# Attention and MLP on one core: the next unit's key part and its copies asked for half a step sooner, and the second pair's bias tiles asked for in units 2 and 3

## The chip, the core and the metric

One NeuronCore of a Trainium2 chip (trn2). Its engines run side by side, each through its own list of instructions in order: TensorE (PE, with its weight loads shown as PEld), VectorE (DVE), ScalarE (ACT), GpSimd (POOL) and SyncE (SP). They wait for each other through semaphores. DMAs are issued here by SP and, for the query part, by POOL. The metric is the device time of one execution in microseconds (us).

## What is computed

Attention over 4 batches, 8 heads, 576 positions and a head size of 64, with a position bias that a small network computes, followed by a two-layer network on the 2304 tokens:

```python
scores = scale * np.matmul(q, k.transpose(0, 1, 3, 2))
h = np.maximum(x @ w1 + b1, 0.0)          # x: log distance over log position, per pair of positions
bias = h @ w2                             # one value per head
scores = scores + bias.transpose(2, 0, 1)[None, :, :, :]
scores = scores - np.max(scores, axis=-1, keepdims=True)
attn = np.exp(scores)
attn = attn / (np.sum(attn, axis=-1, keepdims=True) + 1e-09)
out = np.matmul(attn, v)
...
h = x @ w_in                              # 2304 x 512 by 512 x 2048
g = np.where(h >= 1, h, np.where(h <= -1, 0.0, (h + 1) ** 2 / 4))
y = g @ w_out                             # 2304 x 2048 by 2048 x 512
```

All values are float32. The kernel splits the operands of most products into a rounded high part and a remainder, the low part, and adds the products of the parts.

## The kernel before

**Stages.** From 0 to about 70 us the bias is computed for all heads and stored to DRAM (`bias_d`). From about 70 to 345 us the attention runs. The rest is the two-layer network (lines L678 to L710), with its weights and the start of its input prepared while the attention ends.

**Units, pairs and steps.** The attention is a loop over 16 units. Unit n is one pair of heads (p = n // 4) and one batch (b = n % 4), so the first pair is units 0 to 3 and the second is units 4 to 7. A unit works through five row blocks, k = 0 to 4: four of 128 rows for both heads, and one (named `S_L`, `e_L`, `T_L`) with the last 64 rows of both. For each block:

- TensorE makes the scores S from the keys and the query (L431 and L432; L452 and L453 for the last block), into one of two buffers in PSUM;
- DVE adds the bias tile and finds the row maximum (L434, L454), which frees the buffer;
- ACT takes the exponential (L441);
- TensorE transposes e (T, L497), and the result is split into hi and lo. For some pieces ACT and DVE do that (L472, L473). For five pieces a unit ACT copies T to a tile c (L477), DVE or POOL makes hi (L481 on DVE, L479 on POOL), and POOL subtracts: lo = c - hi (L482). Those five are the second head of block 0, both heads of block 2 and both heads of block 3. POOL makes hi itself for block 0 and for the first head of block 3.

The value products O (L535, L537) are made per half unit, first from hi and then from lo, for the first head and then for the second. The second half of unit n (blocks 2, 3 and the last; tiles `hi_1` and `lo_1`) is multiplied in the first part of unit n + 1.

**The parts of the next units.** `prep(n)` gives eight steps for unit n: 0, load the raw keys and queries (`qk`, L157, on SP); 1, load the query part twice (`qa`, L153, issued by POOL); 2, load the values (`v`, L165, on SP); 3, the high part of the keys (`kh`, a DVE copy, L149); 4, the high part of the values (`vs`, DVE, L161); 5 and 6, the remainder `ls` of the keys in two column halves (POOL, L131), each followed by two DMAs on SP that copy the remainder into the query tile (L176) and the high part of the keys into the other 64 partitions (L177); 7, the remainder of the values (POOL, L131). The scores of unit n need the copies of steps 5 and 6.

**What sets the order.** `CFG["t"]` gives each step a time. A unit has ten half-steps, two per row block, the first behind the block's scores and the second behind its transposes. A time from 0 to 9 places the step of unit n at that half-step of unit n - 2, a time from 10 to 19 at that half-step less 10 of unit n - 1. `STEPS` sorts them, and `step` (called twice per block) runs those that are due. For unit 1, the steps with a time under 10 run during the bias stage. `LB` gives for the five bias tiles of the next pair the batch and the block at which each is asked for; tile 4 is `biasL`. A scheduler then orders each engine's instructions by what it holds to be ready and may move one ahead of where the program has it. On POOL the instructions that go through the helper `pool` keep their program order in the loop; the DVE copies of steps 3 and 4 are kept in order only outside it (`early`). On SP a DMA that waits holds up all behind it.

```python
if t == 20 - 10 * m + i_ and 0 < n + m < N:
    preps[n + m][i]()
```

Of the kernel before, what the change touches and what calls it, by code (L numbers as in the profile page):

```python
# [24 lines left out]
NG = S // 16  # L25
# [3 lines left out]

CBW = (1, 1, 32, C, C, C * H, S // 4, NG)  # L30
CB = sum(CBW)
CFG = dict(un=('paaa',) * NG, xa=((((14, 0), (14, 1), '', 'p'), ((14, 2), (14, 4), '', 'p'), ((14, 4), (15, 0), '', 'p'), ((14, 3), (15, 1), 'bias', 'p')), (((15, 0), (15, 1), 'kh', 'p'), ((15, 0), (15, 2), 'kl', 'v'), ((15, 1), (15, 3), 'vs', 'p'), ((15, 1), (15, 4), '', 'v'))), ex=(9, 2, 0, 2, 9), bb=5, mv=1, hi='pvvpv', rb='a', lag=(1, 1), dr=(3, 1, 2, 2, 2), pool=((0, 1), (2, 0), (2, 1), (3, 0), (3, 1)), sb=4, keep=1, drain=2, diag='a', rb2='v', eps='v', rc=2, rbb=1, hb=2, rawb=(2, 2), t=(3, 10, 11, 10, 18, 11, 12, 19), eb=4, seq=0, pb=(6, 9, 12, 14, 16), pq=22, tb=6, ub=12, low0='ppp', anch=(8, 8, 16, 23, 23), low1='ppp', ob=6, gb=3, fin=2, wt=((15, 1), (15, 4)), lastp=15, xs=2, sbf=('v', 'v', 'v', 'v', 'v'), bsE=(), ytail='p')
EPS = 1e-9
RB = 2
LASTP = CFG["lastp"]
XA = CFG["xa"]
NX = [((14, 0), (14, 1), (14, 1), (15, 0)), ((4, 0), (6, 0), (8, 0), (10, 0))]
WT = CFG["wt"]
LB = ((1, 1), (2, 1), (3, 2), (3, 3), (2, 3))
POOL, SB, KEEP, RBB = CFG["pool"], CFG["sb"], CFG["keep"], CFG["rbb"]  # L40
STEPS = sorted((t, i) for i, t in enumerate(CFG["t"]))
BIG = 3.0e38
# [4 lines left out]
def attn_cpb_moe_kernel(ctx, tc, qk, vL, cb, win, wout, lw, ident, ii, out):  # L47
# [22 lines left out]
    lp = ctx.enter_context(tc.tile_pool(name="a_load", side="right", bufs=2))  # L70
    bp = loads.enter_context(tc.tile_pool(name="a_bias", side="right", bufs=CFG["bb"]))
    qp = loads.enter_context(tc.tile_pool(name="a_qkv", side="right", bufs=2))
# [116 lines left out]
    with ExitStack() as ph:  # L189
# [21 lines left out]
        diag = [ac.tile([P, P], F32, name=f"diag{i}") for i in range(2)]  # L211
# [6 lines left out]
        pq = cp.tile([P, 2, C, H], F32, name="pq")  # L218
# [110 lines left out]
    xs = {}  # L329
# [63 lines left out]
    with ExitStack() as ph:  # L393
# [8 lines left out]
        def load_bias(p, k):  # L402
            if k < 4:
                if (p, k) in ((1, 1), (2, 3)):
                    t = rps[0].tile([P, 3, TH], F32, tag="x", name=f"bias{p}_{k}", bufs=1).rearrange("p a b -> p (a b)")
                else:
                    t = bp.tile([P, 2 * S], F32, tag="bias", name=f"bias{p}_{k}")
                nc.sync.dma_start(out=t[:, 0:S], in_=bias_r[k][:, 2 * p, :])
                nc.sync.dma_start(out=t[:, S : S + D], in_=bias_r[k][:, 2 * p + 1, 512:S])
                nc.sync.dma_start(out=t[:, S + D : 2 * S], in_=bias_r[k][:, 2 * p + 1, 0:512])  # L410
            else:
                t = bp.tile([P, S], F32, tag="biasL", name=f"biasL{p}", bufs=2)
                for j in range(2):
                    nc.sync.dma_start(out=t[D * j : D * j + D, :], in_=bias_r[4][:, 2 * p + j, :])
            return t
# [72 lines left out]
        def transposes(n, k, es, eT):  # L488
            hi, lo = eT
            off = P * (k % 2)  # L490
            e = es[k]
            if k < 4:
                for j in range(2):
                    ps = psT.tile([P, 4, P], F32, tag="T", name=f"T{n}_{k}_{j}")
                    for tb in range(4):
                        c0 = 640 * j + P * tb
                        nc.tensor.transpose(ps[:, tb, :], e[:, c0 : c0 + P], id_s)  # L497
                    split(ps, hi[:, 4 * j : 4 * j + 4, off : off + P], lo[:, 4 * j : 4 * j + 4, off : off + P], EV(n, k, j), (k, j))
            else:
                ps = psT.tile([P, 4, 2, D], F32, tag="T", name=f"T{n}_L")  # L500
                for tb in range(4):
                    nc.tensor.transpose(ps[:, tb].rearrange("p a b -> p (a b)"), e[:, P * tb : P * tb + P], id_s)
                for j in range(2):
                    split(ps[:, :, j, :], hi[:, 4 * j : 4 * j + 4, 256:320], lo[:, 4 * j : 4 * j + 4, 256:320], EV(n, k, j), (k, j))
# [43 lines left out]
        bias = {0: [load_bias(0, k) for k in range(5)]}  # L548
# [4 lines left out]
        def drain(keep, mid=None, at=0):  # L553
            while len(queue) > keep:
                at -= 1
                if at == 0:
                    mid()
                for f in queue.pop(0):
                    f()
# [10 lines left out]
        def step(i_):  # L570
            store_x()
            for m in range(3):
                for t, i in STEPS:
                    if t == 20 - 10 * m + i_ and 0 < n + m < N:
                        preps[n + m][i]()

        go[0] = True
        for n in range(N):
            p, b = n // B, n % B
            if n + 2 < N:  # L580
                preps[n + 2] = prep(n + 2)
            es[n] = []
            if n >= LASTP:
                go[0] = False
            for k in range(5):
                e, later = scores(n, k, qkv[n], bias[p])
                es[n].append(e)
                exps = [False]

                def exp_():  # L590
                    if not exps[0]:
                        exps[0] = True
                        for f in later:
                            exps.append(f())

                if CFG["ex"][k] == 0:
                    exp_()
                step(2 * k)
                if p + 1 < NP:
                    for k_ in range(5):  # L600
                        if (b, k) == LB[k_]:
                            bias.setdefault(p + 1, {})[k_] = load_bias(p + 1, k_)

                def tr(n=n, k=k):
                    half = k // 2 if k < 4 else 1
                    if k in (0, 2):
                        w = 256 + D * half
                        eT[n, half] = (
                            (tp0, tp1)[half].tile([P, 9, w], F32R, tag=f"hi{half}", name=f"hi{n}_{half}"),
                            (tp0, tp1)[half].tile([P, 9, w], F32R, tag=f"lo{half}", name=f"lo{n}_{half}"),  # L610
                        )
                    transposes(n, k, es[n], eT[n, half])
                    if k in (1, 4):
                        shared(n, half, es[n], eT[n, half])

                def inv(n=n):
                    nc.vector.reciprocal(out=sums[n], in_=sums[n])

                def rc(n=n):
                    recips(n)  # L620

                if k in (1, 4):
                    def av(n=n, half=0 if k == 1 else 1):
                        values(n, half, es[n], eT[n, half], qkv[n]["v"])
                    queue.append([tr, inv] if k == 4 else [tr])
                    late.append([CFG["lag"][0 if k == 1 else 1], [av] if k == 1 else [av, rc]])
                else:
                    queue.append([tr])
                while late and late[0][0] <= 0:
                    queue.append(late.pop(0)[1])  # L630
                for x in late:
                    x[0] -= 1
                drain(CFG["dr"][k], exp_, CFG["ex"][k])
                exp_()
                last_e = exps[-1]
                step(2 * k + 1)
                for i in range(NK):
                    for j in range(2):
                        ask, make, home, e = XA[j][i]
                        if (n, k) == ask:  # L640
                            r = None
                            if home:
                                po, w, n_ = dict(kh=(qp, QW, CFG["hb"]), kl=(qp, QW, 2), vs=(qp, 10 * P, 2), bias=(bp, 2 * S, CFG["bb"]))[home]
                                r = po.tile([P, w], F32, tag=home, name=f"rx{j}_{i}", bufs=n_)
                                r = r[:, : 3 * TH].rearrange("p (a b) -> p a b", a=3)
                            xe[i, j] = split_x(0, i, j, e, r)
                        if (n, k) == make:
                            xe[i, j]()
                for f in range(2):
                    if (n, k) == WT[f]:  # L650
                        with tc.issue_after(last_e.ins):
                            weights(f)
# [166 lines left out]
```

## Time and profile before

| | |
|---|---|
| median of 3 runs | 764.74 us (762.58, 764.74, 770.16) |
| the profiled execution's own time | 770.81 us |
| its span, first to last instruction | 769.0 us |
| TensorE busy, share of the span | 717.0 us, 93% |
| ACT, DVE, POOL busy | 62%, 58%, 55% |
| mean granted clock of TensorE, as a share of full speed | 0.984 |
| attention, units 0 to 15 | about 70 to 345 us |
| scores waiting for kh<-kh | 4.2 us in 4 waits |

The profile is one execution. Times in it are us from the span's start. A timeline row is: start, duration, engine, line and operation, out<-in by the program's names, shapes, how many instructions were merged (x4), and in brackets how long the engine had been idle before and for what. For several merged instructions the duration is that of the whole run. SPq is SP's issuing of DMAs, and the duration there is that of the issue, not of the transfer. A busy TensorE row is modelled from starts, so starts are what to compare.

### The profile page before, as it was taken

Reading aid. Unit: us, or ns where it says so; the run is one execution under the profiler, and the core shown is the slowest. Engines: PE = TensorE matmul, PEld = TensorE weight load, DVE = VectorE, ACT = ScalarE, POOL = GpSimd, SP = SyncE. Lnnn points to the kernel's source line nnn. Section 1 sums busy time; section 2 is a strip of 40 time slices with the busy share of each in tenths; the row PEclk is TensorE's granted clock in tenths of the full one; section 3 lists DMA queues with packets and bytes.
Section 4 is the critical chain, followed back from the end, with each engine's and each line's share of the span. In section 5 each row is a group of like instructions: output and inputs, shape, how many; then the busy total and the mean of one; then the engine's idle time right before and its main releaser. Section 6 shows DMA issues by size and latency. Waiting matters only on the chain. (4 is left out here: it accounts for less than half of the span.)

```text
span 769.0 us, 13382 instructions
## 1 busy us (share of the span) xinstructions
PE 717.0 (93%) x4688; PEld 635.8 (83%) x4688; DVE 445.7 (58%) x907; ACT 475.1 (62%) x1041; POOL 419.6 (55%) x362
## 2 busy tenths in 40 slices
PE   5677899899999999787899999999999999999997
PEld 2324899899999999775888889999998999989996
DVE  6998788778878888574665734663222243222222
ACT  7996889879989899596798562432222243222222
POOL 8985688858887888864688442222222222222221
PEclk9999999999999999898999999999999999999999
DMA  8887878956987887437665422461000011000002
GB/s 241 264 250 234 228 186 216 259 152 154 277 233 184 230 188 180 117 100 236 203 218 168 147 94 82 117 180 43 1 1 0 1 40 64 0 1 1 1 0 83
DMA packets 58515, 103.35 MB, mean 134 GB/s; under 512 B 12480, under 2 KB 32464, under 8 KB 58448
## 3 DMA queue, kind: packets, MB, share of 16 engines
q1 hardware_dynamic: 56000, 92.44, 41.7%
q0 software_dynamic: 2304, 9.96, 6.4%
q8 instruction: 37, 0.61, 0.4%
q14 instruction: 30, 0.25, 0.1%
q10 hardware_dynamic: 144, 0.09, 0.1%
HBM read 67.38 MB, written 25.12 MB: 120 GB/s over the span
## 5 line engine op out<-in xcount | busy, mean ns | idle before, releaser
L691 POOL TENSOR_TENSOR gl<-c,gh 128x384 fp32r<-128x384 f32 x96 | 100.7, 1049 | 243.1 <-ACT gh L690 222.3
L688 ACT ACTIVATE c<-c,half_s 128x384 f32<-128x384 f32 x96 | 59.0, 615 | 158.0 <-DVE c L687 157.4
L687 DVE TENSOR_SCALAR c<-h 128x384 f32<-128x384 f32 x96 | 53.2, 554 | 140.0 <-PE h L680 132.6
L482 POOL TENSOR_TENSOR lo<-c,hi 128x512 fp32r<-128x512 f32 x75 | 103.0, 1387 | 44.4 <-DVE hi L481 42.0
L678 PE MATMUL h<-xh,wi 128*128 128x384 f32 x352 | 120.1, 341 | 7.1 <-DVE c L689 4.3
L680 PE MATMUL h<-xh,wi 128*128 128x384 f32 x352 | 118.8, 338 | 0.5 <-POOL wi L118 0.5
L679 PE MATMUL h<-xl,wi 128*128 128x384 f32 x352 | 118.4, 336 | 0.3 <-DVE xl L387 0.3
L699 PE MATMUL y<-wo,gh 128*128 128x512 f32 x288 | 112.7, 393 | 2.6 <-ACT wo L117 2.6
L701 PE MATMUL y<-wo,gl 128*128 128x512 f32 x288 | 114.8, 399 | 0.0
L700 PE MATMUL y<-wo,gh 128*128 128x512 f32 x288 | 114.7, 398 | 0.0
L434 DVE CUSTOM_DVE_ANT_0 e<-S,bias 128x576 f32<-128x576 f32 x128 | 94.8, 751 | 23.6 <-PE S L432 22.2
L441 ACT ACTIVATE e<-e,mx 128x576 f32<-128x576 f32 x128 | 100.5, 787 | 11.5 <-DVE mx L434 11.3
L431 PE MATMUL S<-kh,qa 128*128 128x288 f32 x256 | 79.0, 327 | 7.8 <-DMA kh<-kh 4.2
L689 DVE TENSOR_TENSOR c<-h,c 128x384 f32<-128x384 f32 x96 | 53.3, 556 | 54.9 <-ACT c L688 54.7
L690 ACT CAST gh<-c 128x384 fp32r<-128x384 f32 x96 | 49.1, 512 | 52.6 <-DVE c L689 51.7
L678 PEld LDWEIGHTS h<-xh,wi 128*128 128x128 f32 x352 | 66.1, 188 | 15.8 <-DVE c L689 8.9
L432 PE MATMUL S<-ls,qa 128*128 128x288 f32 x256 | 74.4, 308 | 0.0
L497 PE MATMUL T<-id_s,e 128*128 128x128 f32 x512 | 69.3, 277 | 3.7 <-ACT e L441 3.7
L679 PEld LDWEIGHTS h<-xl,wi 128*128 128x128 f32 x352 | 66.1, 188 | 2.9 <-DVE xl L387 0.5
L680 PEld LDWEIGHTS h<-xh,wi 128*128 128x128 f32 x352 | 66.0, 188 | 0.9 <-POOL wi L118 0.8
L699 PEld LDWEIGHTS y<-wo,gh 128*128 128x128 f32 x288 | 54.6, 190 | 11.7 <-ACT wo L117 2.9
L701 PEld LDWEIGHTS y<-wo,gl 128*128 128x128 f32 x288 | 54.6, 190 | 11.6
(121 smaller groups left out, 1521.7 us busy)
## 6 DMA issues: line engine op xcount, KB each, us to landing
bias_d<-y SPq DMA_DIRECT2D x36, 295.5 KB, 4.6
qk<-in_qk_dram SPq DMA_DIRECT2D x16, 608.0 KB, 4.9
qa<-in_qk_dram POOLq DMA_DIRECT2D x16, 608.0 KB, 7.1
rawi<-in_win_dram SPq DMA_DIRECT2D x16, 512.0 KB, 4.1
rawo<-in_wout_dram SPq DMA_DIRECT2D x16, 512.0 KB, 3.8
x<-xT SPq DMA_DIRECT2D x40, 192.0 KB, 3.5
v<-in_vL_dram SPq DMA_DIRECT2D x16, 320.0 KB, 3.9
qa<-ls SPq DMA_DIRECT2D x32, 152.0 KB, 4.8
```

Of the source, the lines that this page charges most:

```text
L431: nc.tensor.matmul(ps[:, hf, :HS], qs[:, qc], kh[:, kc : kc + HS], start=True, stop=False)
L432: nc.tensor.matmul(ps[:, hf, :HS], q0[:, qc], kl[:, kc : kc + HS], start=False, stop=True)
L434: nc.vector.tensor_tensor_reduce(out=ev.rearrange("p (a b) -> p a b", a=2), in0=ps[:, :, :HS], in1=bias[k][:, S * j : S * j + S].rearrange ...
L441: lambda ev=ev, j=j: nc.scalar.activation(ev, ev, AF.Exp, bias=mx[:, j : j + 1], scale=-1.0, accum_out=sm[:, 4 * j + k : 4 * j + k + 1])
L482: r = nc.gpsimd.tensor_tensor(out=lo, in0=m, in1=hi.bitcast(F32), op=ALU.subtract)
L678: nc.tensor.matmul(ps[:, :TH], wh_, xh, start=k == 0, stop=False)
L679: nc.tensor.matmul(ps[:, :TH], wh_, xl, start=False, stop=False)
L680: nc.tensor.matmul(ps[:, :TH], wl_, xh, start=False, stop=k == NK - 1)
L691: nc.gpsimd.tensor_tensor(out=gl, in0=c, in1=gh.bitcast(F32), op=ALU.subtract)
L699: nc.tensor.matmul(y, gh[:, c], wo[f][0], start=f == 0, stop=False)
L700: nc.tensor.matmul(y, gh[:, c], wo[f][1], start=False, stop=False)
L701: nc.tensor.matmul(y, gl[:, c], wo[f][0], start=False, stop=f == NF - 1)
```

## The change

`CFG["t"]` is changed in three of its eight times. Step 3 (the high part of the keys) goes from 10 to 9: from half-step 0 of the unit before to the last half-step of the unit before that. Steps 5 and 6 (the two key remainders with their four DMAs) go from 11 and 12 to 10 and 11. `LB` becomes a list with one entry per pair. For the second pair it asks for tiles 0, 1 and 4 at (2, 0), (2, 3) and (3, 0), where they were asked for at (1, 1), (2, 1) and (2, 3). Tiles 2 and 3, and the later pairs, are as they were.

```diff
-CFG = dict(... t=(3, 10, 11, 10, 18, 11, 12, 19), ...)
+CFG = dict(... t=(3, 10, 11, 9, 18, 10, 11, 19), ...)
...
-LB = ((1, 1), (2, 1), (3, 2), (3, 3), (2, 3))
+LB = [((2, 0), (2, 3), (3, 2), (3, 3), (3, 0))] + [((1, 1), (2, 1), (3, 2), (3, 3), (2, 3))] * 2
...
-                        if (b, k) == LB[k_]:
+                        if (b, k) == LB[p][k_]:
```

What stands where on the engines is given by the built programs. First POOL in the round in which unit 4's scores are made, before. `hi_1` and `lo_1` are the second half of unit 4, `ls_2757` is the key remainder of unit 6; `vs_2684` and `qa_111` are unit 5's values and unit 6's query tile.

```order
L131 TENSOR_TENSOR vs_2684<-v_2509,vs_2684 128x10x64
L153 DMA qa_111<-in_qk_dram 64x2x1216
L479 CAST hi_1_2650<-c_2739 128x4x128
L482 TENSOR_TENSOR lo_1_2651<-c_2739,hi_1_2650 128x4x128
L482 TENSOR_TENSOR lo_1_2651<-c_2748,hi_1_2650 128x4x128
L131 TENSOR_TENSOR ls_2757<-qk_2598,kh_2732 128x608 x2
L479 CAST hi_0_2800<-c_2814 128x4x128
```

The same place in the changed program; the key remainder is `ls_2734` there.

```order
L131 TENSOR_TENSOR vs_2684<-v_2513,vs_2684 128x10x64
L153 DMA qa_111<-in_qk_dram 64x2x1216
L131 TENSOR_TENSOR ls_2734<-qk_2598,kh_2716 128x608
L479 CAST hi_1_2650<-c_2743 128x4x128
L482 TENSOR_TENSOR lo_1_2651<-c_2743,hi_1_2650 128x4x128
L482 TENSOR_TENSOR lo_1_2651<-c_2752,hi_1_2650 128x4x128
L131 TENSOR_TENSOR ls_2734<-qk_2598,kh_2716 128x608
L479 CAST hi_0_2800<-c_2814 128x4x128
```

One of the two remainders has moved ahead of the cast and the two lo tiles of block 3, and the other has stayed. The same holds for units 2 to 15's remainders, in units 0 to 13's rounds.

Next SP around the start of unit 4, before: `v_2755` is unit 6's values, the bias tiles belong to the third pair (units 8 to 11), and `ls_2511` and `kh_2486` are unit 5's key copies.

```order
L165 DMA v_2755<-in_vL_dram 128x640
L568 DMA xT_2_64<-x_0_2440 256x1x256
L408 DMA bias_1_3029<-bias_d_58 128x576
L409 DMA bias_1_3029<-bias_d_58 128x64
L410 DMA bias_1_3029<-bias_d_58 128x512
L414 DMA biasL_3151<-bias_d_61 64x576 x2
L176 DMA qa_112<-ls_2511 64x608
L177 DMA kh_2486<-kh_2486 64x608
L176 DMA qa_112<-ls_2511 64x608
L177 DMA kh_2486<-kh_2486 64x608
L524 DMA rT_3_77<-r_2595 9x128
```

The same place in the changed program, from the bias tile's last piece on.

```order
L410 DMA bias_1_3029<-bias_d_58 128x512
L414 DMA biasL_3151<-bias_d_61 64x576
L176 DMA qa_112<-ls_2488 64x608
L177 DMA kh_2470<-kh_2470 64x608
L176 DMA qa_112<-ls_2488 64x608
L177 DMA kh_2470<-kh_2470 64x608
L157 DMA qk_2848<-in_qk_dram 128x1216
L524 DMA rT_3_77<-r_2595 9x128
L568 DMA xT_2_64<-x_1_2568 256x1x320
L414 DMA biasL_3151<-bias_d_61 64x576
```

One of the two `biasL` loads has moved from ahead of unit 5's copies to behind them, and the raw load `qk` has moved ahead of the stores rT and xT. Last SP at the start of unit 1, before: `bias_0_1773` is the second pair's tile 0, `qk_1843` unit 3's raw load, and `kh_1547` unit 1's key copy.

```order
L177 DMA kh_1547<-kh_1547 64x608
L408 DMA bias_0_1773<-bias_d_57 128x576
L409 DMA bias_0_1773<-bias_d_57 128x64
L410 DMA bias_0_1773<-bias_d_57 128x512
L157 DMA qk_1843<-in_qk_dram 128x1216
```

The same place in the changed program.

```order
L177 DMA kh_977<-kh_977 64x608
L157 DMA qk_1839<-in_qk_dram 128x1216
L408 DMA bias_0_1979<-bias_d_57 128x576
L409 DMA bias_0_1979<-bias_d_57 128x64
L410 DMA bias_0_1979<-bias_d_57 128x512
```

The tile that is asked for in unit 1 before, and in unit 2 after, stands at the same place in both but for the raw load, which is now ahead of it. On DVE the key copies (L149) of units 1 and 2 alone have moved: unit 1's into the bias stage, unit 2's ahead of the first two evictions of unit 1.

## Rows read from the trace of the kernel before

**Rows 1.** Table of stretches: span, then busy us per engine, clock, DMA share, GB/s.
```profile
70.00:100.00 30.00, 26.46 (x192) 24.91 (x192) 22.96 (x56) 22.71 (x58) 18.27 (x15) 0.94 0.81 217
140.00:160.00 20.00, 17.35 (x121) 16.50 (x120) 13.15 (x31) 14.70 (x38) 14.23 (x12) 0.91 0.97 237
160.00:300.00 140.00, 138.55 (x1072) 133.97 (x1071) 116.18 (x269) 127.18 (x333) 114.47 (x95) 1.00 0.80 201
```
**Rows 2.** Timeline of POOL, block 3 of unit 2 and what precedes it.
```profile
116.59 3.10 POOL L482 TENSOR_TENSOR lo<-c,hi 128x512 fp32r<-128x512 f32 x2 [2.40 <-DVE hi L481]
...
121.15 0.62 POOL L153 DMA_DIRECT2D qa<-in_qk_dram  x1
121.78 0.63 POOL L479 CAST hi<-c 128x512 fp32r<-128x512 f32 x1
122.49 2.54 POOL L482 TENSOR_TENSOR lo<-c,hi 128x512 fp32r<-128x512 f32 x2
124.99 1.51 POOL L131 TENSOR_TENSOR ls<-qk,kh 128x608 fp32r<-128x608 f32 x1
```
**Rows 3.** Timeline of TensorE, the first O<-lo of unit 2's second half.
```profile
124.83 0.75 PE L535 MATMUL O<-lo,vs 128*128 128x320 f32 x4
```
**Rows 4.** POOL's lo (85 to 300 us) and ls (90 to 310): ns min/median/max.
```profile
L482 POOL TENSOR_TENSOR lo<-c,hi x67: 1276/1293/1848, 83.8 to 298.7; 128x512 fp32r<-128x512 f32 x67
...
L131 POOL TENSOR_TENSOR ls<-qk,kh x28: 1466/1500/1746, 94.4 to 308.2; 128x608 fp32r<-128x608 f32 x28
```
**Rows 5.** Timeline of POOL, the lo tiles of block 3 in units 0, 1, 7, 12.
```profile
91.84 2.55 POOL L482 TENSOR_TENSOR lo<-c,hi 128x512 fp32r<-128x512 f32 x2
...
106.54 2.55 POOL L482 TENSOR_TENSOR lo<-c,hi 128x512 fp32r<-128x512 f32 x2
...
207.31 2.53 POOL L482 TENSOR_TENSOR lo<-c,hi 128x512 fp32r<-128x512 f32 x2
...
287.41 2.54 POOL L482 TENSOR_TENSOR lo<-c,hi 128x512 fp32r<-128x512 f32 x2
```
**Rows 6.** Timeline of TensorE, the first scores of units 1 and 5.
```profile
82.65 0.37 PE L431 MATMUL S<-kh,qa 128*128 128x288 f32 x1 [1.45 <-DMA kh<-kh]
...
152.58 0.38 PE L431 MATMUL S<-kh,qa 128*128 128x288 f32 x1 [2.13 <-DMA kh<-kh]
```
**Rows 7.** Timeline of TensorE, the first O<-lo of units 0, 1, 7, 12.
```profile
93.22 0.82 PE L535 MATMUL O<-lo,vs 128*128 128x320 f32 x4
...
108.55 0.75 PE L535 MATMUL O<-lo,vs 128*128 128x320 f32 x4
...
210.13 0.75 PE L535 MATMUL O<-lo,vs 128*128 128x320 f32 x4
...
289.74 0.75 PE L535 MATMUL O<-lo,vs 128*128 128x320 f32 x4
```
**Rows 8.** Timeline of DVE: unit 2's key copy, and a values cast in unit 3.
```profile
88.35 0.79 DVE L149 CAST kh<-qk 128x1216 fp32r<-128x1216 f32 x1
...
127.23 1.07 DVE L161 CAST vs<-v 128x640 fp32r<-128x640 f32 x1 [1.07 <-PE O L537]
```
**Rows 9.** Timelines of ACT and TensorE behind unit 13's products.
```profile
310.61 0.51 ACT L383 CAST xh<-rx 128x384 fp32r<-128x384 f32 x1 [2.80 <-POOL rx L379]
...
311.50 0.69 PE L511 MATMUL T_s<-id_s,e 128*128 128x128 f32 x2 [2.33 <-ACT x L538]
```
**Rows 10.** SP's issues: unit 1's first key copy, unit 5's query and key copies.
```profile
78.31 0.60 SPq L177 DMA_DIRECT2D kh<-kh  x1
...
142.48 0.49 SPq L176 DMA_DIRECT2D qa<-ls  x1
146.59 0.49 SPq L177 DMA_DIRECT2D kh<-kh  x1
```
**Rows 11.** Waits in SP's queue, 137 to 149 us: total us, times, longest.
```profile
SPq L177 <- DMA v<-in_vL_dram: 3.6, 1, 3.6
```
**Rows 12.** The DMA view of 137 to 152 us.
```profile
DMA packets 2066, 3.48 MB, mean 232 GB/s; under 512 B 515, under 2 KB 964, under 8 KB 2064
```

More of the change, by code (lines that the diff above doesn't have):

```diff
@@ L31 @@
 CB = sum(CBW)
-CFG = dict(un=('paaa',) * NG, xa=((((14, 0), (14, 1), '', 'p'), ((14, 2), (14, 4), '', 'p'), ((14, 4), (15, 0), '', 'p'), ((14, 3), (15, 1), 'bias', 'p')), (((15, 0), (15, 1), 'kh', 'p'), ((15, 0), (15, 2), 'kl', 'v'), ((15, 1), (15, 3), 'vs', 'p'), ((15, 1), (15, 4), '', 'v'))), ex=(9, 2, 0, 2, 9), bb=5, mv=1, hi='pvvpv', rb='a', lag=(1, 1), dr=(3, 1, 2, 2, 2), pool=((0, 1), (2, 0), (2, 1), (3, 0), (3, 1)), sb=4, keep=1, drain=2, diag='a', rb2='v', eps='v', rc=2, rbb=1, hb=2, rawb=(2, 2), t=(3, 10, 11, 10, 18, 11, 12, 19), eb=4, seq=0, pb=(6, 9, 12, 14, 16), pq=22, tb=6, ub=12, low0='ppp', anch=(8, 8, 16, 23, 23), low1='ppp', ob=6, gb=3, fin=2, wt=((15, 1), (15, 4)), lastp=15, xs=2, sbf=('v', 'v', 'v', 'v', 'v'), bsE=(), ytail='p')
+CFG = dict(un=('paaa',) * NG, xa=((((14, 0), (14, 1), '', 'p'), ((14, 2), (14, 4), '', 'p'), ((14, 4), (15, 0), '', 'p'), ((14, 3), (15, 1), 'bias', 'p')), (((15, 0), (15, 1), 'kh', 'p'), ((15, 0), (15, 2), 'kl', 'v'), ((15, 1), (15, 3), 'vs', 'p'), ((15, 1), (15, 4), '', 'v'))), ex=(9, 2, 0, 2, 9), bb=5, mv=1, hi='pvvpv', rb='a', lag=(1, 1), dr=(3, 1, 2, 2, 2), pool=((0, 1), (2, 0), (2, 1), (3, 0), (3, 1)), sb=4, keep=1, drain=2, diag='a', rb2='v', eps='v', rc=2, rbb=1, hb=2, rawb=(2, 2), t=(3, 10, 11, 9, 18, 10, 11, 19), eb=4, seq=0, pb=(6, 9, 12, 14, 16), pq=22, tb=6, ub=12, low0='ppp', anch=(8, 8, 16, 23, 23), low1='ppp', ob=6, gb=3, fin=2, wt=((15, 1), (15, 4)), lastp=15, xs=2, sbf=('v', 'v', 'v', 'v', 'v'), bsE=(), ytail='p')
 EPS = 1e-9
```

## Prediction

> **What bounds the kernel now.** I read the table of stretches first. From 160 to 300 us, which is most of the attention loop, TensorE is busy 138.55 of 140 us at the full 2.4 GHz (granted clock 1.00), and no other engine comes near that [rows 1]. The reader is to see that a unit there is as long as TensorE's own work, so that work taken from other engines gains nothing, and that anything TensorE has to stand still for is added in full. The exception is the stretch from 140 to 160 us: 2.65 us of it idle, at a mean granted clock of 0.91 [rows 1]. The timeline of TensorE shows what it stands for: the first scores of unit 5 wait 2.13 us for the copy of the keys (the DMA kh<-kh) [rows 6]. So I looked in two places: what the change does to that copy, and what it does to the four engines in an ordinary unit, eight or more times over.
>
> In an ordinary unit the timeline of POOL is the one to read. In unit 2's round it waits 2.40 us for DVE's hi at 116.59, does two remainders lo, then vs, then the query DMA (issued at 121.15), the cast hi of row block 3 at 121.78, the two remainders lo of block 3 from 122.49, and only at 124.99 the key remainders ls of the unit after next [rows 2]. TensorE reads the first of these lo tiles in the product O<-lo of unit 2's second half, which starts at 124.83 [rows 3] (that half's products run in the first part of the next unit). A lo takes 1.29 us and an ls 1.50 us [rows 4], so that lo is ready at 123.78: 1.05 us before it is read.
>
> **The change, part by part.**
>
> *The key remainders (steps 5 and 6).* The order of POOL shows it in every unit: one ls now stands between the query DMA and the cast hi, the other stays behind the lo tiles. In unit 2's round the ls takes the slot at 121.78, and hi, lo and lo start 1.50 us later. Nothing hides it: the 2.40 us that POOL stands idle lie ahead of this place, and the ls cannot slip into them, since it is behind lo, vs and the query DMA in the queue. The first lo then ends at 122.49 + 1.50 + 1.29 = 125.28; TensorE follows a POOL result after about 0.09 us (unit 0: lo ends at 91.84 + 1.29 = 93.13, the product starts at 93.22 [rows 4, 5, 7]), so it starts at 125.37 and not at 124.83: **0.54 us of standing**. What is queued behind that product is all of TensorE's work, the next unit's transposes too. The second lo comes 1.25 us behind the first (124.99 less 122.49, over two), and TensorE has ten matmuls to do between the two products, of which four take 0.75 us [rows 3]; so only the first lo costs.
>
> Is it given back later in the unit? DVE's cast of vs at 127.23 has itself waited 1.07 us for TensorE's O products [rows 8], and DVE's evictions of the next scores stand behind it; so DVE moves back with TensorE, and so does POOL, whose round begins with a wait for DVE [rows 2]. I take nothing back; the other bound is all of it.
>
> The same sum, (start of lo + 2.88) minus start of the product, for the other units [rows 5, 7]: unit 0: 91.84 + 2.88 - 93.22 = 1.50; unit 1: 106.54 + 2.88 - 108.55 = 0.87; unit 12: 287.41 + 2.88 - 289.74 = 0.55. Units 2, 3, 5, 6, 9, 10, 11 and 12 agree to 0.02 us (the first and the last stand here). In units 4, 7 and 8 there is room: 207.31 + 2.88 - 210.13 = 0.06 for unit 7, which I take as nothing. In unit 13 the product is late too, but TensorE stands 2.33 us a little later anyway, for ACT, which itself waited 2.80 us for POOL's work on the network's input, and the place of that work behind both ls is unchanged [rows 9]: nothing.
>
> *The key copy on DVE (step 3).* From unit 3 on DVE's order is what it was. Unit 2's cast, 0.79 us [rows 8], goes ahead of two evictions at the start of unit 1, so scores of unit 1 lose up to 0.8 us; but the product of unit 0 that comes right behind is held by POOL to 94.72, 1.50 us late, and the two delays overlap. Counted in the 1.50. Unit 1's cast leaves the start of the loop. That would gain some 0.8 us, but TensorE then waits for unit 1's key copy, 1.45 us at 82.65 today [rows 6]; SP issues that copy at 78.31 [rows 10], from a place in its queue that has not moved behind stores and bias loads. A gain ahead of that wait is lost in it: nothing.
>
> *SP's queue.* The four part copies of a unit keep their places; the raw load qk passes the stores rT and xT, which are read only from unit 14 on, for the network's input; and in unit 1 it passes three pieces of a bias tile that is first used some 50 us on. An issue is 0.5 us, hidden by those times: nothing.
>
> *The bias tiles.* The request list for the second pair changes, but SP's order puts the first tile of it where it was, behind unit 1's copies (it is hoisted ahead of its request in both kernels). So this part moves no transfer worth naming.
>
> *The start of unit 5.* Here the second half of a biasL load goes from ahead of the part copies to behind the raw load. Before, the query part is issued at 142.48, and the key copy only at 146.59, since it waited 3.6 us for the load of v to land [rows 10, 11]. v is the eighth DMA ahead of it in the queue, and in the changed order the eighth ahead is a piece of a bias tile from before v; so the issue may come up to 3.6 us sooner. But in 137 to 152 us the DMA engines carry 3.48 MB at 232 GB/s [rows 12], and the copy has the same queue of loads ahead of it whenever it is issued, less 64 x 576 x 4 = 147 KB. That is 147 KB / 232 GB/s = 0.63 us. The lower bound is nothing, the upper bound the whole 2.13 us.
> The Trainium skill ("DMA: Bandwidth & Descriptors", section "Issuing engines are not separate DMA queues") says that transfers issued by any engine run on the same 16 DMA engines and interleave, which speaks against gaining by an earlier issue here. By that rule the term is the 0.63 us; by the issue times alone it would be 2.13 us and the sum 1.5 us less. The 232 GB/s row bears the rule out.
> I take 0.63 us, nearest to a queue that is full. The 0.55 us of unit 3 falls into this wait and is not counted.
>
> **Sum.** 1.50 + 0.87 + 7 x 0.55 (units 2, 5, 6, 9, 10, 11, 12) - 0.63 = **+5.6 us**. The profiled execution took 770.81 us, the median of three is 764.74; the sum is made on the former and carried over to the latter: 770.3 us, +0.7%.
>
> **The rivals.**
> - *DVE gives the loop's part back* (its evictions catch up while TensorE stands): 7 x 0.55 = 3.85 us less, 766.5 us. For it: in the loop some scores do wait for evictions. Against: the 1.07 us that DVE itself waits [rows 8].
> - *Unit 5's gate opens fully.* The copy lands as much sooner as it is issued: 2.13 us, and with the gap the lower clock goes. 0.91 as a mean of 1.2 and 2.4 GHz is 18% of 20 us, 3.6 us, at half speed, or 1.8 us lost. 3.93 gained, 1.50 + 0.87 + 8 x 0.55 = 6.77 lost: +2.8, 767.6 us. For it: the sooner issue. Against: the bytes ahead.
> - *Nothing of it shows*: POOL's room is larger than its rows say (an ls shorter than the 1.05 us of room): 764.74 - 0.63 = 764.1 us. Against: 28 ls of a median of 1.50.
> - *The other side, clearly slower: the clock.* Standing 1.50 us at 93 us and 0.87 us at 108 us could bring the lower clock, as the stretch from 140 to 160 has it; each such stretch costs the 1.8 us worked out above, two 3.6: 773.9 us. It decides from about 2 us more than my sum. Against: from 70 to 100 us TensorE stands 3.54 us already, and the mean of 0.94 there is 12% of 30 us, one such stretch and no more [rows 1].
>
> **How the numbers follow.** My forecast 0.45; DVE gives back 0.15; unit 5 opens 0.17; nothing 0.08; clock 0.15. About 1% (7.6 us) is what a measurement of this kernel tells from no change: the three times lie 7.6 us apart. The forecast is within it by 2 us, so part of its spread and most of the clock case count as slower: 0.20; faster needs more gain than any case has: 0.02; the same: 0.78. Range 764.0 to 775.0 us: from the case of nothing to the clock case and 1 us for units 4, 7 and 8, should they lose their room.
>
> **What would show it.** Right: in the changed kernel's timelines the first O<-lo of a unit begins some 0.1 us behind POOL's first lo, TensorE waits there by 0.5 us for POOL, and units of the loop are about 16.5 us long; the wait of unit 5's scores for kh<-kh is smaller, not gone. Wrong: TensorE goes on without that wait, or units are as long as before; or the wait at unit 5 is gone altogether. An extra stretch at half clock would show in the row PEclk.

## The result, and the profile after

| | before | after |
|---|---|---|
| median, beside each other on one chip | 766.94 us (762.58 to 770.16) | 773.71 us (770.43 to 778.43) |
| ratio, 95% interval | | 1.0094 (1.0069 to 1.012) |
| ratio on another chip (run a2 below) | | 1.0056 (1.003 to 1.0083) |
| profiled execution, and its span | 770.81 us, 769.0 us | 771.92 us, 770.1 us |
| TensorE busy; mean granted clock | 717.0 us; 0.984 | 717.1 us; 0.987 |
| ACT, DVE, POOL busy | 62%, 58%, 55% | 62%, 57%, 54% |
| scores waiting for kh<-kh | 4.2 us in 4 waits | 4.0 us in 6 waits |

The change costs 0.9% in the first measurement and 0.6% in the second: 6.8 and 5.0 us of median. The two profiled executions differ by only 1.1 us, since that of before was one of its slowest. So it is the lengths of the units that are to be compared, not the spans.

The table of stretches of after (columns as in [rows 1]).

```profile
70.00:100.00 30.00, 27.29 (x193) 25.20 (x192) 21.97 (x54) 23.63 (x61) 15.61 (x14) 0.94 0.86 241
140.00:160.00 20.00, 18.36 (x130) 17.73 (x129) 13.72 (x34) 15.64 (x42) 15.51 (x14) 0.91 1.02 241
160.00:300.00 140.00, 136.76 (x1056) 131.88 (x1055) 112.28 (x267) 124.80 (x325) 110.76 (x92) 1.00 0.81 198
```

From 160 to 300 us TensorE is now idle for 3.24 us, where it was 1.45; the clock is the same in all three stretches. The timeline of POOL in unit 2, against [rows 2], and of TensorE behind it, against [rows 3]:

```profile
115.79 3.10 POOL L482 TENSOR_TENSOR lo<-c,hi 128x512 fp32r<-128x512 f32 x2 [2.61 <-DVE hi L481]
120.99 1.50 POOL L131 TENSOR_TENSOR ls<-qk,kh 128x608 fp32r<-128x608 f32 x1
122.43 0.61 POOL L479 CAST hi<-c 128x512 fp32r<-128x512 f32 x1
123.12 2.55 POOL L482 TENSOR_TENSOR lo<-c,hi 128x512 fp32r<-128x512 f32 x2
```

```profile
123.88 0.30 PE L537 MATMUL O<-hi,vs 128*128 128x320 f32 x1
124.47 0.86 PE L535 MATMUL O<-lo,vs 128*128 128x320 f32 x4 [0.28 <-POOL lo L482]
```

The remainder stands where the order put it, and TensorE begins 0.06 us behind the first lo (123.12 + 1.29 = 124.41). In unit 12 [rows 5, 7] it is the same: lo from 290.03, the product at 291.39. The first scores of units 1 and 5, against [rows 6], and the products behind unit 13, against [rows 9]:

```profile
80.12 0.38 PE L431 MATMUL S<-kh,qa 128*128 128x288 f32 x1
...
151.26 0.37 PE L431 MATMUL S<-kh,qa 128*128 128x288 f32 x1 [0.58 <-DMA kh<-kh]
...
153.10 0.48 PE L431 MATMUL S<-kh,qa 128*128 128x288 f32 x1 [1.07 <-DMA kh<-kh]
...
312.88 0.44 PE L511 MATMUL T_s<-id_s,e 128*128 128x128 f32 x2 [0.95 <-ACT x L538]
```

Unit 1 no longer waits for its keys, and unit 5 waits 0.58 and 1.07 us where it waited 2.13 and, 1.20 us further on, another 0.43:

```profile
153.78 0.37 PE L431 MATMUL S<-kh,qa 128*128 128x288 f32 x1 [0.43 <-DMA kh<-kh]
```

SP issues unit 5's copies sooner than in [rows 10], the first key copy by 5.5 us (4.9 us, if both are counted from unit 4's first scores):

```profile
140.34 0.61 SPq L176 DMA_DIRECT2D qa<-ls  x1
141.04 0.55 SPq L177 DMA_DIRECT2D kh<-kh  x1
145.35 0.46 SPq L176 DMA_DIRECT2D qa<-ls  x1
145.87 0.59 SPq L177 DMA_DIRECT2D kh<-kh  x1
```

TensorE's waits in the whole execution (total us, times, longest) have a line that before has not; its longest is in unit 14:

```profile
PE S L431 <- DMA kh<-kh: 4.0, 6, 1.1
...
PE O L535 <- POOL lo L482: 3.3, 8, 1.1
```

The lengths of the units, first scores to next first scores, in three pairs of profiles (b2 and a2 are before and after once more; pin_b and pin_a are told below):

| unit | before | after | b2 | a2 | pin_b | pin_a |
|---|---|---|---|---|---|---|
| 0 | 12.88 | 11.31 | 12.87 | 11.09 | 10.70 | 10.06 |
| 1 | 19.44 | 21.17 | 20.03 | 20.00 | 18.74 | 20.43 |
| 2 | 16.29 | 16.30 | 16.33 | 16.27 | 16.33 | 16.28 |
| 4 and 5 | 36.98 | 36.14 | 31.69 | 33.94 | 31.92 | 32.26 |
| 8 and 9 | 32.20 | 33.96 | 32.79 | 33.95 | 31.91 | 32.27 |
| 10 to 13, each | 15.93 to 15.95 | 16.12 to 16.15 | 15.93 to 15.97 | 16.12 to 16.15 | 15.94 to 15.95 | 16.12 to 16.14 |
| 14 | 22.96 | 23.96 | 22.75 | 24.08 | 22.78 | 23.09 |
| unit 0 to unit 15 | 252.43 | 255.80 | 248.80 | 252.31 | 244.02 | 247.90 |

An undisturbed unit, one in which no wait for a DMA falls, is 0.18 us longer, not 0.55. The attention is 3.4, 3.5 and 3.9 us longer in the three pairs. What the medians of the first two pairs have beyond that (6.8 less 3.4, and 5.0 less 3.5 us) lies in no place that these profiles show alike: single executions of either kernel lie up to 8 us apart.

### The profile page after: what moved, and what is told of

Its sections match the earlier page's. It is cut to its first block, busy times and chain, and to the rows that moved or that the text cites. A ratio compares the mean times of both kernels' runs of the same rounds, so it can differ in the third digit from the quotient of the medians.

```text
span 770.1 us, 13398 instructions
## 1 busy us (share of the span) xinstructions
PE 717.1 (93%) x4688; PEld 635.1 (82%) x4688; DVE 440.2 (57%) x907; ACT 475.0 (62%) x1041; POOL 419.4 (54%) x362
## 5 line engine op out<-in xcount | busy, mean ns | idle before, releaser
L431 PE MATMUL S<-kh,qa 128*128 128x288 f32 x256 | 77.3, 321 | 7.2 <-DMA kh<-kh 4.0
L497 PEld LDWEIGHTS T<-id_s,e 128*128 128x128 f32 x512 | 60.0, 145 | 5.3 <-ACT e L441 5.1
```

What stands on the lines that cost most here:

```text
L431: nc.tensor.matmul(ps[:, hf, :HS], qs[:, qc], kh[:, kc : kc + HS], start=True, stop=False)
```

## The experiments

All ratios are against before on the same chip, with a 95% interval.

**Before again (b2).**

> The kernel before, run once more under another name: a ratio of 1.000, within 0.003 either way, and a second profile of it. It shows how far a measurement of this size can be trusted, and which of the waits in the first profile of before return.

0.9999 (0.9969 to 1.0029). Unit 5's waits are not in this profile, nor is the stretch at the lower clock behind them (units 4 and 5 are 5.3 us shorter), while undisturbed units are 15.95 us again. So the wait of [rows 6] comes and goes between executions, and the length of an undisturbed unit does not.

**Step 3 alone (key).** `t=(3, 10, 11, 9, 18, 11, 12, 19)`, the old LB.

> Only step 3 of t is changed (10 to 9), with the old bias list: POOL's order is that of before, and DVE's key copies of units 1 and 2 stand where the change has them. Theory (POOL's key remainder ahead of block 3's lo tiles makes the loss): no loss here, a ratio of 0.997 to 1.001. Rival (the early key copy on DVE makes it): about 1.009. The earlier copy of unit 1's keys may take away TensorE's wait at unit 1 (1.45 us in before), which would be 0.998.

1.0005 (0.9978 to 1.0031), undisturbed units of 15.94 to 15.97 us: no loss. TensorE still waits at unit 1.

**Steps 5 and 6 alone (parts).** `t=(3, 10, 11, 10, 18, 10, 11, 19)`, the old LB.

> Only steps 5 and 6 of t are changed (11, 12 to 10, 11), with the old bias list: POOL's order is that of the changed kernel, and one key remainder (1.50 us) stands ahead of block 3's hi and lo tiles in each unit. Theory (POOL): the whole loss or a little more, a ratio of 1.008 to 1.012 (6 to 9 us), TensorE's first O<-lo of a half 0.06 us behind POOL's lo, and units of the loop 0.1 to 0.3 us longer than before. Rivals (the key copy, or the bias list): 1.000 to 1.002.

1.0068 (1.0037 to 1.0098), undisturbed units of 16.12 to 16.15 us; the ratio is a little below the 1.008 that I had as the least. Without step 3, unit 1 begins as in the changed kernel, with no wait for its keys. Unit 0 is 10.71 us; its mean granted clock is 1.00 in this profile, 0.87 in before and 0.85 in after, so its length is not to be compared with theirs.

**The list alone (lb).**

> Only the list of the bias tiles is changed. The orders of the five engines differ from before in two rows of SP alone. Theory: no difference, a ratio of 0.998 to 1.002. Rival (the list makes what steps 5 and 6 alone leave over, 1.0094 less 1.0068): 1.002 to 1.004.

0.9993 (0.9966 to 1.0019). POOL's order makes the loss; the key copy and the list do not.

**The change again (a2).**

> The changed kernel, run once more: a ratio of 1.009 (1.006 to 1.012), and a second profile of it. The regular units of the loop should be 16.13 us again, against 15.95 in before; the starts of units 1, 4, 5, 8 and 9, where TensorE waits for the DMA kh<-kh, should differ from the first profile of the changed kernel, if it is the traffic of the DMA engines that sets them.

1.0056 (1.003 to 1.0083), just under my range, and 16.12 to 16.15 us a unit. The waits for kh<-kh are 3.1 us where the first profile has 4.0, and lie elsewhere in part.

**The bias loads held back (pin_b on before, pin_a on the change).** Each load of `load_bias` for a later pair is kept on SP behind what the program has ahead of it.

```diff
+            keep = tc.keep_in_program_order if p else lambda ins: ins
...
-                nc.sync.dma_start(out=t[:, 0:S], in_=bias_r[k][:, 2 * p, :])
+                keep(nc.sync.dma_start(out=t[:, 0:S], in_=bias_r[k][:, 2 * p, :]))
```

> Before, with the bias loads of the later pairs held on SP behind what the program has ahead of them, so that they are issued where the list LB asks and not hoisted to the start of a pair; all other engines keep their order. It tests the step on unit 5. If the copy of unit 5's keys is late for the bytes ahead of it in the DMA engines (some 1 MB of bias tiles), the wait of 2.1 us at unit 5 goes, with the stretch at half clock behind it: a ratio of 0.993 to 0.998. If it is late for its own issue or latency, the wait stays and the ratio is 1.000.

0.9965 (0.9937 to 0.9993). Unit 5 begins at 146.58 us here. The DMA views from unit 4's first scores to unit 5's, in before and in pin_b; in pin_b, SP's issues of unit 5's copies; the landing of the query copies, recorded for one of the two, in before and in pin_b (KB each, us); and TensorE's waits from 125 to 230 us in pin_b (total us, times, longest):

```profile
DMA packets 2454, 4.60 MB, mean 252 GB/s; under 512 B 550, under 2 KB 1039, under 8 KB 2452
...
DMA packets 1892, 3.92 MB, mean 246 GB/s; under 512 B 337, under 2 KB 924, under 8 KB 1890
```

```profile
138.74 0.51 SPq L176 DMA_DIRECT2D qa<-ls  x1
139.34 0.55 SPq L177 DMA_DIRECT2D kh<-kh  x1
```

```profile
qa<-ls SPq DMA_DIRECT2D x2, 152.0 KB, 6.0
...
qa<-ls SPq DMA_DIRECT2D x2, 152.0 KB, 3.2
```

```profile
PE S L432 <- DMA kh<-kh: 0.2, 1, 0.2
```

Unit 5's wait is gone, and units 3 to 13 are all 15.94 to 15.97 us. So the bias loads ahead of them made the keys late, but in two ways that this run does not part. SP issues the first key copy 0.60 us behind the query copy, where in before it stood 3.6 us for the landing of v [rows 10, 11]; and 0.7 MB less are carried in that unit, and the query copy lands in 3.2 us instead of 6.0. The bytes alone do not decide: b2 carries 4.58 MB in the same stretch and does not wait at unit 5. Once more (pin_b2):

> pin_b once more, beside the three above on one chip: a ratio of 0.9965 (0.994 to 0.999), regular units of 15.95 us, and no wait for kh<-kh at units 4, 5, 8 and 9.

0.9972 (0.9952 to 0.9992). Units 3, 4, 7 and 8 are 0.2 to 0.8 us longer in this profile, with one wait of 0.3 us for kh<-kh, at unit 8, where I had expected none; the others from 3 to 13 are 15.93 to 15.97 us.

> The changed kernel with the bias loads held on SP as in pin_b. Against pin_b it is the change without the waits for the DMA engines. If POOL's order alone makes the loss of 7 us, it is all here: 0.9965 + 0.0094 = 1.006. If the order costs only the 0.18 us by which the profile shows each regular unit longer, and the rest are waits for kh<-kh: eleven units by 0.18 us and 1.5 us at unit 1 are 3.5 us, a ratio of 1.000 to 1.002. My prediction's 0.55 us a unit without anything given back would be 6 to 8 us more than pin_b: 1.005 to 1.007.

1.0002 (0.9978 to 1.0026), as the second reading of the expectation had it. With the bias loads held, the change costs 3.9 us of the attention's length, 1.69 of it in unit 1 and 0.18 in each undisturbed unit from 4 on, and some 0.003 to 0.004 in the ratio. That the waits for DMAs make the rest of the full loss is likely (units 4, 5, 8 and 9 of a2 are together 3.4 us longer than those of b2, and those of pin_a 0.7 longer than those of pin_b), but it is not shown: the same four units of after are only 0.9 us longer than those of before, and the intervals of the ratios are wide.

**Both remainders ahead (dose2).** `t=(3, 10, 11, 10, 18, 10, 10, 19)`.

> Both key remainders ahead of block 3's hi and lo tiles on POOL, where the change has one (steps 5 and 6 both at 10; the rest as before). The first lo of a half comes another 1.5 us later. If what a unit can give back is a fixed slack (the 0.37 us that the change has used up already), the whole 1.5 us shows in each unit: regular units of 17.6 us, eleven to fourteen units by 1.6 us, a ratio of 1.025 to 1.035. If two thirds of any such wait are given back in the unit: units of 16.6 us, and 1.012 to 1.018. If POOL's order is not the cause at all: 1.007.

1.0352 (1.0318 to 1.0387). A table of stretches by unit, units 5 to 8:

```profile
155.00:172.84 17.84, 16.22 (x126) 15.36 (x125) 13.29 (x32) 14.65 (x39) 13.07 (x12) 1.00 0.64 162
172.84:191.96 19.12, 17.60 (x126) 16.79 (x125) 12.91 (x32) 14.63 (x39) 13.03 (x12) 0.91 0.59 147
191.96:209.77 17.81, 16.24 (x126) 15.39 (x124) 13.31 (x32) 14.64 (x39) 13.04 (x12) 1.00 0.83 198
209.77:227.59 17.82, 16.21 (x126) 15.35 (x124) 13.30 (x32) 14.64 (x39) 13.05 (x12) 1.00 0.94 264
```

The second remainder costs 1.69 us a unit (17.82 less 16.13) where the first cost 0.18, so what a unit gives back is a fixed amount, used up by the first. Units 3, 6, 9 and 12 are another 1.3 us longer, each with a mean granted clock of 0.91: a part of each ran at the lower level, 1.2 GHz.

**A small remainder ahead (half).** pin_a with the remainders cut at a quarter.

```diff
-                c = slice(QW // 2 * i, QW // 2 * i + QW // 2)
+                c = slice(0, QW // 4) if i == 0 else slice(QW // 4, QW)
```

> pin_a with the two key remainders cut unevenly: 304 columns in the one that stands ahead of block 3's hi and lo tiles, 912 in the one behind them (608 each in pin_a). The first should take half of 1.50 us, 0.75 us, which is less than the 1.05 us by which POOL's lo was early in before. If a remainder ahead costs only what exceeds that room, TensorE's wait for lo goes, and regular units are 15.95 us again, as in pin_b: a ratio of 0.995 to 0.999. If any work put ahead of the lo tiles costs in proportion: 16.04 us, and 0.999 to 1.000.

1.0021 (1.0 to 1.0043). Timeline of POOL in unit 10, then TensorE's waits from 68 to 345 us:

```profile
236.51 0.84 POOL L131 TENSOR_TENSOR ls<-qk,kh 128x304 fp32r<-128x304 f32 x1
237.30 0.61 POOL L480 CAST hi<-c 128x512 fp32r<-128x512 f32 x1
237.99 2.56 POOL L483 TENSOR_TENSOR lo<-c,hi 128x512 fp32r<-128x512 f32 x2
```

```profile
PE S L432 <- DMA kh<-kh: 7.5, 5, 2.4
```

The unit is 15.93 to 15.95 us again: 0.84 us ahead of the lo tiles fits in the room of 1.05 us and costs nothing. The ratio was missed all the same: 7.5 us of waiting for kh<-kh, at units 1, 3, 4, 8 and 13. The copy that comes second now carries 912 of the 1216 columns, nearly half of the first head's keys among them, and TensorE needs it earlier: at unit 3 it stands behind the first of four groups of scores (119.51 us), in pin_a behind the second (117.03). Which of the two, the size or the earlier need, weighs more is not tested. I had asked only what POOL's order does, and not what the cut does to the DMAs that follow.

**Where 0.37 us a unit is given back.** The timelines of DVE and POOL in unit 10, before:

```profile
244.32 1.08 DVE L161 CAST vs<-v 128x640 fp32r<-128x640 f32 x1 [1.07 <-PE O L537]
245.32 0.75 DVE L434 CUSTOM_DVE_ANT_0 e<-S,bias 128x576 f32<-128x576 f32 x1
```

```profile
242.09 2.96 POOL L131 TENSOR_TENSOR ls<-qk,kh 128x608 fp32r<-128x608 f32 x2
```

and after:

```profile
245.47 0.51 DVE L161 CAST vs<-v 128x640 fp32r<-128x640 f32 x1 [1.62 <-PE O L537]
245.90 0.74 DVE L434 CUSTOM_DVE_ANT_0 e<-S,bias 128x576 f32<-128x576 f32 x1
```

```profile
244.14 1.49 POOL L131 TENSOR_TENSOR ls<-qk,kh 128x608 fp32r<-128x608 f32 x1
```

The cast waits 0.55 us longer for TensorE and then takes 0.51 us, where it took 1.08. In both it ends 0.35 us behind POOL's remainder (245.40 against 245.05; 245.98 against 245.63). So in before the cast was started at 244.32 but held until POOL was done, and the 0.54 us that TensorE loses vanish in that hold: counted from the unit's first scores, the eviction behind the cast begins 9.84 us in before and 9.81 us after. What stays is 0.17 us: ACT's hi of block 1, which did move back by 0.54, now reaches DVE 0.17 us too late for the lo of the same block, and the rest of the round follows.

Two runs move that cast behind the next eviction (vk14_b on pin_b, vk14_a on pin_a).

```diff
-            early(nc.vector.tensor_copy(a["v"][:, :, 0:D], a["rv"]))
+            c_ = nc.vector.tensor_copy(a["v"][:, :, 0:D], a["rv"])
+            if n > 1:
+                tc.keep_in_program_order(c_)
+            else:
+                early(c_)
```

with step 4 at 14 in `t`.

> pin_b with DVE's cast vs held behind the eviction of S_2_1 (step 4 at 14, kept in program order). In pin_b that cast takes 1.07 us and ends 0.35 us behind POOL's key remainder, with the eviction of S_2_1 queued behind it. If it is POOL's remainder that holds the cast, it takes 0.4 to 0.55 us in its new place, where POOL has finished, the eviction comes 0.5 to 0.7 us sooner, TensorE's waits for evictions in blocks 3 and 4 go, and regular units are 15.6 to 15.9 us: 0.991 to 0.997. If the cast takes about 1 us in itself, the next work on DVE comes as late as before: units of 15.95 us or longer, 0.996 or more.

0.9957 (0.9933 to 0.9981), 762.84 us: undisturbed units of 15.38 to 15.59 us. DVE and then POOL in unit 10:

```profile
235.15 0.76 DVE L439 CUSTOM_DVE_ANT_0 e<-S,bias 128x576 f32<-128x576 f32 x1 [1.31 <-PE S L437]
235.83 0.49 DVE L161 CAST vs<-v 128x640 fp32r<-128x640 f32 x1
```

```profile
232.99 2.96 POOL L131 TENSOR_TENSOR ls<-qk,kh 128x608 fp32r<-128x608 f32 x2
235.88 0.91 POOL L484 CAST hi<-c 128x512 fp32r<-128x512 f32 x1
```

The same cast takes 0.49 us here, begun when POOL's remainders have 0.12 us left (232.99 + 2.96 = 235.95), and the unit is shorter by 0.36 to 0.57 us. Units 7 and 11 are 1.5 and 1.2 us longer than these, with waits of 1.43 and 0.93 us for kh<-kh at their ends, and the units after them 0.9 each, so the ratio cannot be told from that of pin_b.

> pin_a with the same move of DVE's cast vs. In pin_a TensorE stands 0.54 us for POOL's lo, and units are only 0.18 us longer than in pin_b. If what gives the rest back is the cast (it starts 0.54 us later, but ends when POOL's remainder lets it, at the same time as in pin_b), then with the cast moved away nothing can give it back, and units are 0.4 to 0.55 us longer than in vk14_b, a ratio 0.008 to 0.010 above that of vk14_b. If the rest is given back elsewhere (by TensorE's own waits for evictions), the difference stays at 0.1 to 0.2 us a unit, and 0.003 to 0.005 in the ratio.

1.0159 (1.0133 to 1.0185): units of 17.19 us, 1.7 us longer than those of vk14_b, and not 0.4 to 0.55. DVE and POOL in unit 10:

```profile
247.77 1.51 DVE L161 CAST vs<-v 128x640 fp32r<-128x640 f32 x1
249.20 0.68 DVE L478 TENSOR_TENSOR lo<-T,hi 128x512 fp32r<-128x512 f32 x1
```

```profile
246.94 0.61 POOL L484 CAST hi<-c 128x512 fp32r<-128x512 f32 x1
247.63 1.30 POOL L487 TENSOR_TENSOR lo<-c,hi 128x512 fp32r<-128x512 f32 x1
```

In its new place the cast falls behind POOL's next lo and is held again, to 0.35 us behind its end (249.28 against 248.93). The hold of 1.0 us (1.51 less 0.49) is about what the unit has more than pin_a's (17.19 less 16.13 = 1.06). So this run did not take the cover away cleanly, as I meant it to, and its expectation failed; it shows the hold itself instead, and what it seems to cost when nothing else covers it.

## Why the prediction was right, and where it was not

The forecast was +5.6 us, 770.3 us, within 1%. Measured were +6.8 and +5.0 us, 773.71 us inside the range. The cause is the one named, but several terms of the sum were wrong, in opposite directions.

- **TensorE bounds the loop; POOL's remainder holds O<-lo.** Right. parts shows it alone, dose2 and half show its dose: 0.84 us ahead adds nothing to a unit, 1.50 us adds 0.18, 3.0 us adds 1.87.
- **0.54 us of standing in an ordinary unit.** Right: in unit 10 the products of the second head begin 0.54 us later, counted from the unit's first scores (pin_a against pin_b). 0.43 of them stand ahead of the first O<-lo; the four products behind that wait then take 0.86 us instead of 0.75.
- **"I take nothing back."** Wrong, and the largest error. The 0.55 us counted for seven units is 0.18, and it falls in all of units 3 to 13 that no DMA disturbs: about 2.0 us (11 x 0.18) for 3.85. I took DVE's wait for TensorE [rows 8] as proof that DVE moves back as a whole. But DVE's cast had a second holder, POOL's remainder, and that one had not moved. The rival "DVE gives the loop's part back" was nearer; two thirds of it is true, by another way than the one given there. The room that I gave units 4, 7 and 8 was that of one profile, in which waits had made their products late: 6.85 us behind the next unit's first scores for unit 7, and 6.44 in pin_b, where no DMA disturbs it.
- **Unit 0: 1.50 us; unit 1: 0.87 us.** The first is right in two pairs of three: 1.69 us in pin_a, 1.73 in after, in the length of unit 1. In the pair of b2 and a2 unit 1 is as long in both (20.03 and 20.00), where b2 stood 0.90 us for DVE's last eviction. The second is given back whole: unit 2 is 16.30 us, and was 16.29.
- **The wait for unit 1's keys stays.** Wrong: it went, with a gain of 1.6 us in unit 0 (0.6 between pin_b and pin_a, neither of which waits there). The key copy on DVE did not open it (key keeps the wait, 1.47 us), the earlier remainders alone may (parts has lost it); but the wait is no fixed cost either, since b2 has 0.61 us of it, and lb and pin_b, in the old order of POOL, have none. I had looked only at the raw key copy's place.
- **Unit 5: 0.63 us.** Right in kind: the copy was asked for 5.5 us sooner and the waits went from 2.56 us (2.13 + 0.43) to 1.65 (0.58 + 1.07), smaller and not gone. pin_b shows that the bias loads ahead make them; that it is their bytes and not SP's queue, as I had it, is not shown. And it is no fixed cost: in b2 it is missing.
- **Key copy on DVE, bias list: nothing.** Right (key, lb).
- **Unit 13: nothing.** The wait behind it fell from 2.33 to 0.95 us and the product took 1.1 us of waiting for lo, as argued. But unit 14 as a whole is 1.0 and 1.3 us longer in the two profiles of the change, 0.3 in pin_a and not at all in parts. Of the 1.0 and 1.3 us, 0.9 and 1.2 lie at the unit's end, behind its wait for ACT's e, where TensorE is busy without a break. The stretches from there to unit 15's first scores, in before and in after:

```profile
316.57:322.21 5.64, 5.63 (x32) 5.45 (x33) 4.01 (x10) 4.30 (x11) 2.83 (x4) 0.70 0.42 120
...
318.10:324.60 6.50, 6.50 (x32) 6.50 (x33) 4.00 (x10) 4.29 (x11) 3.69 (x4) 0.56 0.55 146
```

  The same part takes 6.6 us at a clock of 0.55 in a2, and 5.5 to 5.6 us at 0.69 or 0.70 in b2, pin_b, pin_a and parts. So what unit 14 has more is time at the lower clock; POOL's order alone does not bring it, since pin_a and parts have that order too.
- **Units 8 and 9, not foreseen.** 1.8 us longer in after, 1.2 in a2, for waits for kh<-kh, where my text had room. The keys are asked for sooner there (unit 9's first copy 7.3 us behind unit 8's first scores, 10.7 in before), and land no sooner: the scores of unit 9 wait 1.06 us for them where they waited 0.23. What makes them late there was not tested apart from pin_a.
- **The clock.** Not in the loop: after has no stretch below 1.00 from 160 to 300 us, and unit 5 has 0.91 in both kernels. But most of unit 14's part of the loss is the clock's, as told above, and the 3.0 us of dose2 bring the lower level in every third unit, for 1.3 us each where I had worked out 1.8.

So the total came out near by luck, by errors that cancel: 1.9 us too much for the loop and 0.9 for unit 1's second half, some 0.6 to 1.6 us of gain ahead of unit 1 not seen, and 2.5 to 2.8 us too little for units 8, 9 and 14. The profiles account for 3.4 to 3.9 us of the loss; the rest of the medians' 5.0 to 6.8 us stays without a place.

The lowest ratio here is that of vk14_b, before with the bias loads held back and the cast moved: 0.9957; the interval does not part it from pin_b. The change itself is not worth keeping.

## What to carry to other kernels

Before you say that a delay is passed on, look at what the delayed instruction does after its start: where one operation on one shape has durations of 0.49 and 1.07 us, the longer one may be held by another engine, and then a late start costs nothing up to the holder's end. Put work into an engine's queue by the room that the trace shows behind it, and read that room in a unit that no other wait has stretched. Expect no price up to there, and the whole price only where every such cover further on is used up too: here 0.84 us cost nothing, the first 1.50 cost 0.18, and the next 1.50 cost 1.69. A transfer asked for sooner need not land sooner: look at what stands ahead of it.

## What was not expected of the hardware

DVE's cast vs (128 x 640, fp32) takes 0.49 us where POOL is idle (at 239.96 us in dose2). Where an instruction of POOL is running when it starts, it ends 0.35 us behind that instruction: 1.08 us beside a remainder in before, 0.97 beside a lo in dose2, 1.51 beside a lo in vk14_a. Where that instruction has hardly 0.1 us left, the cast takes its 0.49 us and ends 0.37 to 0.42 us behind it. One cast of before, in unit 14, does not fit: it starts at 308.09 us, when a remainder has 0.11 us left, lasts 3.39 us, over the next remainder, rx and a cast hi of POOL, and ends 0.35 us behind the last of them. Why it did not come in between is open. In the other direction POOL's own cast hi takes 0.87 to 0.93 us when it starts beside DVE's cast, and 0.60 to 0.64 otherwise. The rows of the cast that show its spread, before and then after (ns min/median/max):

```profile
L161 DVE CAST vs<-v x13: 494/1073/1578, 95.7 to 292.1; 128x640 fp32r<-128x640 f32 x13
```

```profile
L161 DVE CAST vs<-v x13: 495/510/1480, 94.8 to 293.9; 128x640 fp32r<-128x640 f32 x13
```

The Trainium skill ("SBUF — State Buffer", section "SBUF: two separate sides") says that DVE and GpSimd have one pair of SBUF ports in common, that for the operations which need it the pair is a lock held for a whole instruction, and that the one which comes second is blocked and not slowed. The traces agree: the cast's end follows that of POOL's instruction by 0.35 us, whether the cast began 0.06 us after that instruction (at 163.71 us in before) or 1.33 us after it (unit 10 of after).

Executions of one program differ by 5.3 us at one place: units 4 and 5 take 36.98 us in one profile of before and 31.69 in the other. 2.56 us of it are waits for unit 5's keys, of which the second profile has none, and unit 5 itself has a mean granted clock of 0.91 in the first and 1.00 in the second.
